# Reordering a tuned kernel: the first batch's scores and weight products, w_o's split, ScalarE's order around T1 and T2, and the end

## The chip, the cores and the metric

The kernel runs on one core of a Trainium2 chip. The metric is the time of one execution on the device in microseconds (us); less is better. A core has five engines that run their own queues of instructions in parallel: TensorE (PE: matrix products and transposes into PSUM), VectorE (DVE), ScalarE (ACT), GpSimd (POOL) and SyncE (SP, which here issues nearly all transfers). An instruction that waits holds everything behind it in its engine's queue.

## The reference, cut to what is computed

Eight batches; 8 heads of 576 tokens with 64 dimensions, 32 packed queries per head; model width 512; 4 experts of width 64, two of them chosen per token.

```python
def sm_attn(qq, kk, vv):
    a = softmax(qq @ kk.T / 8)
    return a @ vv
p_packed = sm_attn(p, k, v)                  # 32 rows per head
x = sm_attn(q, p_packed, p_packed)           # 576 rows per head, heads joined to 512

h = gelu_tanh(x @ w_in)                      # 1024 wide
u, v = h[..., :512], h[..., 512:]
v_n = (v - mean) / sqrt(var + 1e-6) * g_ln
v_s = einsum('ts,bsd->btd', w_sg, v_n) + b_sg
x = x + (u * v_s) @ w_out

w = softmax over the 2 largest of x @ w_gate
for e in range(4):
    a = causal softmax((x @ wq[e]) @ (x @ wk[e]).T / 8)
    out += w[e] * (a @ (x @ wv[e]) @ wo[e])
```

## The kernel before

**Precision.** Most products run as three passes over a high and a low part of each operand (hi by hi, hi by lo, lo by hi). Wherever a result is needed as an operand again, ACT copies the high part out of PSUM and DVE or POOL subtracts it to get the low part (`act_copy`, L82; `lo_part`, L85).

**Folding.** w_out is folded into w_qk and w_vg at the start, and the packed attention's result is carried as two factors: the 32 packed rows per head (turned: ppT) and the weights a2. So x is never formed: `bdw` (L636) multiplies the packed rows into w_qk ("bdq", the tile `bdq`) and into w_vg (`bdv`), and q, k, values and gate logits are sums of a gated part (`qk_gated`, L819: 24 products per call from gh, gl and w_qk) and a packed part (`qk_packed`, L831: 12 products from a2h, a2l and bdq). `qk_out` (L843) splits the sum. `vlog` (L860) makes values and gate logits of some token tiles.

**Batches.** `startup` (L1482) does batch 0's front half by a list of steps written out by hand (ORDER). Batch 0's back half is `first_back` (L1118), later ones' `later_back` (L1141); `back` (L1179) joins them with what is common. Each back half also carries the packed attention of the next batch in steps: K0 and K1 turn k's layout, V loads v, s0 and s1 are the scores of p with k (PE product, DVE maximum, ACT exponential; two halves of the heads), n0 and n1 their sums, a0 and a1 their transposes (PE, then a DVE copy, tile `a1t`), p0 and p1 the products with v (tile `pp`), Q0 and Q1 turn q's layout, P0 and P1 the transposed packed rows (`ppT`), and r, among others, the second scores S2 (q with the packed rows) and their softmax. `front(b)` makes v, u and the layer norm of batch b and `wp_mm` the product of the packed rows with w_in.

**Attention of the experts.** Ten items per batch (five token tiles by two pairs of experts). For item i, S is E (scores on PE, DVE's mask and maximum `nm`, ACT's exponentials, tile `at`) and N (DVE's scaling of `at`) together; T is the transposes of `at` on PE (tile `aTp`) and ACT's copies (tile `aT`). y and o, numbered by token tile, are the product with the values and the product with w_o. `vs_tile(b, m)` is the spatial product of column block m (`vs_mm`, 36 products) and `vs_out`: DVE's `gt`, ACT's high part `gh`, DVE's low part `gl`.

**Buffers.** All PSUM tiles come from one pool of four slots (`pd`, L74); a new tile waits until the readers of the oldest free slot's last tile are done. Loads of the natural layout and w_o's staging tile share two slots (`nat_slot`, L71), weights two slots "W" (w_in's halves, w_qk, w_vg), v and others three slots "a".

**What sets the order.** In the startup all five engines follow the order of the code. After it PE and SP do (L1489), and the others' order is made by the scheduler, except inside a `manual_schedule` block for an engine (VectorE's at L1159, L1197 and L1219), where the code's order holds.

**w_o.** `prep_w_o(j)` (L347) loads half of w_o through SP, copies the high part on ACT and subtracts on POOL. It is called at the end of `back(0)` (L1225), and w_o is first used by o0 of batch 0, which stands in batch 1's back half.

Of the kernel before, what the change touches and what calls it, by code (L numbers as in the profile page):

```python
# [26 lines left out]
def packed_attention_mlp_moe_kernel(  # L27
# [46 lines left out]
    def pd(name):  # L74

        return psum.tile([P, 2, 512], F32, tag="pd", name=name, bufs=NPS)
# [7 lines left out]
    def lo_part(eng, o, x, hi):  # L84
        eng.tensor_tensor(o, x, hi.bitcast(F32), op=OP.subtract)  # L85
# [291 lines left out]
    ST = {}  # L377
# [256 lines left out]
        wp_out(b, f)  # L634

    def bdw(b):  # L636

        s = ST[b]
        pt = pd("bdq")
        per_head(b, pt, 512, w_of(b, "qk"))  # L640
        for Q in range(2):
            hi, lo = s["bd", Q] = [slot("B", F32R, 512, name="bdq") for _ in range(2)]
            nc.scalar.activation(hi, pt[:, Q, :], AF.Copy)
            lo_part(nc.vector, lo, pt[:, Q, :], hi)
        pt = pd("bdv")
        per_head(b, pt, 260, w_of(b, "vg"))
        t = [slot("B", F32R, 520, name="bdv").rearrange("p (q n) -> p q n", q=2) for _ in range(2)]
        nc.scalar.activation(t[0], pt[:, :, :260], AF.Copy)
        lo_part(nc.vector, t[1], pt[:, :, :260], t[0])
        for Q in range(2):  # L650
            s["bdv", Q] = [x[:, Q, :] for x in t]
# [450 lines left out]
    def weights(b, names):  # L1102
        if b < B:
            for n in names:
                load_w(n)
# [11 lines left out]

    def first_back(b, do_all):  # L1118
        tick(len(TURN))
        do_all("K0")  # L1120
        qk_gated(b, 0, True)
        do_all("s0 n0 K1 V")
        qk_gated(b, 2, True)
        do_all("s1 n1")
        bdw(b)
        weights(b + 1, ("in1", "in0"))
        do_all("a0")
        qk_packed(b, 0, False)
        qk_out(b, 0)
        do_all("a1 p0 Q0")  # L1130
        qk_packed(b, 2, False)
        qk_out(b, 2)
        keep_last_q(b, 0)
        do_all("P0")
        vlog(b, VT[2])
        do_all("p1 Q1 P1")
        vlog(b, VT[1])
        do_all("r")
        ahead(b + 2)

    def later_back(b, go, do_all, nxt):  # L1141
        go("S1 S3")
        vs_tile(b, 0)
        vs_tile(b, 1)
        go("T1 T2 y0 S5 S4")
        vs_tile(b, 2)
        go("T3 o0 y1 T5 T4 S6 S7")
        vs_tile(b, 3)
        tick(len(TURN))
        if b + 1 < B:  # L1150
            STEP.pop((b + 1, "f"))()
        go("o1 y2")
        bdw(b)
        weights(b + 1, ("in1", "in0"))
        qk(b, 0)
        do_all("V T6 o2 T7 K0 S8 S9 K1")
        keep_last_q(b, 0)
        qk_gated(b, 2, True)
        with tc.manual_schedule(engines={ET.DVE}):  # L1159
            do_all("s0 s1 n0 n1")  # L1160
        qk_packed(b, 2, False)
        qk_out(b, 2)
        if b + 1 == B:
            go("y3 T8 T9 o3 y4")
            nxt("E8")
            go("o4")
            vlog(b, VT[1])
            nxt("E6")
            vlog(b, VT[2])
            nxt("E4")  # L1170
            return
        do_all("y3 T8 T9 o3 a0 a1 y4 p0 Q0 p1 Q1 o4 P0 P1")
        vlog(b, VT[1])
        do_all("r")
        vlog(b, VT[2])
        if b + 2 < B:
            ahead(b + 2)

    def back(b, go):  # L1179
        def do_all(names):  # L1180

            for n in names.split():
                if (b + 1, n) in STEP:
                    STEP.pop((b + 1, n))()
                elif n[0] in "STyo":
                    go(n)

        nxt = attention(b)
        if b:
            later_back(b, go, do_all, nxt)  # L1190
        else:
            first_back(b, do_all)
        vlog(b, VT[0])
        tick()
        gates(b)
        if b + 1 == B:
            with tc.manual_schedule(engines={ET.DVE}):  # L1197
                nxt("N8 N6")
                qk(b, 1)
                keep_last_q(b, 1)  # L1200
                nxt("E2 N4")
                qk_packed(b, 3, True)
                nxt("E0 N2")
                qk_gated(b, 3, False)
                qk_out(b, 3)
                nxt("N0 T8 T0 T2 E9 E1 T4 N9 E3 T6 N1 T9 y4 N3 T1 E5 y0 o4 T3 y1 N5 E7 o0 T5 y2 N7 o1 T7 y3 o2 o3")
            return
        qk(b, 1)
        keep_last_q(b, 1)
        tick()  # L1210
        nxt("E0 E2")
        qk_packed(b, 3, True)
        tick()
        qk_gated(b, 3, False, (0, 1, 2))
        wp_mm(b + 1, 1)
        wp_mm(b + 1, 0)
        qk_gated(b, 3, False, (3,))
        tick()
        with tc.manual_schedule(engines={ET.DVE}):  # L1219
            wp_out(b + 1, 1)  # L1220
            wp_out(b + 1, 0)
            qk_out(b, 3)
            nxt("N0 N2")
        weights(b + 1, ("qk", "vg"))
        if b == 0:  # L1225
            for j in range(2):
                prep_w_o(j)
        return nxt

    def ahead(b):  # L1230
# [294 lines left out]
```

## Time and profile before

| | us |
|---|---|
| median of 3 runs | 844.61 |
| lowest and highest run | 844.15 and 848.43 |
| the profiled execution's own time | 844.43 |
| span from its first to its last instruction | 842.7 |
| outside the span | 1.73 |
| mean granted clock of TensorE over the span | 0.992 |

The profile comes from one execution. Its page gives each engine's busy time; the view of waits says how long an engine stood idle in front of which instruction, and whose result came last; the timeline lists instructions in order of time, with a wait in brackets behind the instruction that waited; the view by windows gives each engine's busy time in a stretch and the clock that was granted to TensorE, as a share of 2.4 GHz. "L772" is a line of the kernel before; "x16" is a count of instructions merged into one row.

### The profile page before, as it was taken

What the parts mean: (1) busy time and instruction counts of PE and PEld (TensorE: products, weight loads), DVE (VectorE), ACT (ScalarE), POOL (GpSimd) and SP (SyncE); (2) the same over time, 40 slices, a digit from 0 to 9 for tenths busy, and PEclk for the clock granted to TensorE, in tenths of its full rate; (3) what the DMA queues carried; (4) which work ended last, traced back from release to release, by engine and by line L of the source; (5) the groups of instructions that cost most, each with busy time, mean ns of one, the idle gap of its engine ahead of it and who ended that gap; (6) DMA issues with size and microseconds to landing.
All of it is one profiled execution on the core that took longest, in us unless ns stands there. A gap on an engine that the chain in (4) does not pass through costs nothing.

```text
span 842.7 us, 19253 instructions
## 1 busy us (share of the span) xinstructions
PE 804.4 (95%) x7523; PEld 695.5 (83%) x7523; DVE 572.3 (68%) x1359; ACT 431.1 (51%) x983; POOL 226.1 (27%) x301
## 2 busy tenths in 40 slices
PE   4689989999999999999999999999999999999988
PEld 2467778788889889888889889888889889888876
DVE  5999546776468846776468856776468856775374
ACT  3655432765347542665346542665346543665344
POOL 2457412403322322303322331303322322300000
PEclk9989999999999999999999999999999999999999
DMA  9977793617555374517565475617654470200001
GB/s 249 284 202 170 221 272 92 190 50 214 141 153 121 95 231 113 165 51 217 136 163 113 101 226 112 160 56 214 147 161 108 99 228 8 76 14 27 19 1 58
DMA packets 172710, 115.00 MB, mean 136 GB/s; under 512 B 119306, under 2 KB 153610, under 8 KB 169804
## 3 DMA queue, kind: packets, MB, share of 16 engines
q1 hardware_dynamic: 165644, 112.19, 49.7%
q10 hardware_dynamic: 6976, 1.58, 0.9%
q8 instruction: 60, 0.98, 0.5%
q14 instruction: 30, 0.25, 0.1%
HBM read 69.18 MB, written 29.63 MB: 117 GB/s over the span
## 4 chain that ended last, share of the span: by engine, by line
PE 59%; DVE 14%; ACT 4%; issue 3%; ACTq 0%
PE qk L828 10%; PE vlog L871 6%; PE vs L772 6%; PE y L1011 6%; PE qk L840 6%; PE o L1060 5%; PE aTp L982 4%; PE vlog L875 3%; PE sc L924 3%; DVE vg L683 2%; DVE bnst L671 2%; DVE vnl L698 2%; PE s L392 2%; PE sc L955 2%; DVE at L943 1%
## 5 line engine op out<-in xcount | busy, mean ns | idle before, releaser
L772 PE MATMUL vs<-w_sg,vnh 128*128 128x288 f32 x512 | 91.7, 301 | 3.4 <-ACT aT L82 1.9
L473 POOL COPY kT<-kp 128x576 uint16<-128x576 uint16 x56 | 50.2, 973 | 157.6 <-DMA kp<-turned_k 132.3
L828 PE MATMUL qk<-gh,w_qk 128*128 128x288 f32 x512 | 90.6, 299 | 0.0
L772 PEld LDWEIGHTS vs<-w_sg,vnh 128*128 128x128 f32 x512 | 74.5, 188 | 10.7 <-issue 3.9
L934 ACT ACTIVATE at<-sc,nm 128x256 f32<-128x256 f32 (+3 forms) x128 | 66.1, 524 | 32.4 <-DVE nm L928 28.6
L828 PEld LDWEIGHTS qk<-gh,w_qk 128*128 128x128 f32 x512 | 74.7, 188 | 9.3 <-issue 9.3
L82 ACT ACTIVATE aT<-aTp 128x512 f32<-128x512 f32 (+4 forms) x160 | 59.3, 434 | 21.1 <-PE aTp L982 17.7
L858 POOL CAST last_q<-qk 64x64 fp32r<-64x64 f32 x64 | 14.9, 232 | 178.4 <-ACT qk L848 101.6
L871 PE MATMUL vlog<-w_vg,gh 128*128 128x260 f32 (+1 forms) x320 | 60.5, 287 | 0.0
L473 POOL COPY qT<-qp 128x576 uint16<-128x576 uint16 x56 | 42.8, 833 | 62.0 <-DMA qp<-turned_q 61.9
L1011 PE MATMUL y<-aT,v 128*64 128x128 f32 (+2 forms) x960 | 57.7, 262 | 0.2 <-DVE y L85 0.2
L679 POOL TENSOR_TENSOR rstd<-rstd,mhalf 128x1 f32<-128x1 f32 x40 | 35.5, 894 | 83.2 <-DVE rstd L675 83.2
L1011 PEld LDWEIGHTS y<-aT,v 128*64 128x64 f32 (+1 forms) x960 | 46.7, 136 | 12.2 <-issue 7.3
L943 DVE TENSOR_SCALAR at<-at,sm,gw 128x256 f32<-128x256 f32 (+3 forms) x128 | 54.8, 470 | 1.6
L828 PE MATMUL qk<-gl,w_qk 128*128 128x288 f32 x256 | 54.8, 296 | 0.0
L772 PE MATMUL vs<-w_sg,vnl 128*128 128x288 f32 x256 | 54.7, 295 | 0.0
L928 DVE TENSOR_REDUCE nm<-sc 128x2 f32<-128x256 f32 (+3 forms) x64 | 52.0, 821 | 1.5
L871 PEld LDWEIGHTS vlog<-w_vg,gh 128*128 128x128 f32 (+1 forms) x320 | 47.2, 178 | 3.9 <-DVE lg L880 2.8
L1060 PE MATMUL o<-w_o,y 128*128 128x512 f32 x186 | 50.0, 404 | 0.0
L840 PE MATMUL qk<-a2h,bdq 128*128 128x288 f32 x256 | 46.8, 305 | 0.0
L982 PE MATMUL aTp<-ident,at 128*128 128x128 f32 x320 | 43.6, 274 | 2.7 <-DVE at L943 2.3
L871 PE MATMUL vlog<-w_vg,gl 128*128 128x260 f32 (+1 forms) x160 | 45.1, 282 | 0.0
(237 smaller groups left out, 1922.9 us busy)
## 6 DMA issues: line engine op xcount, KB each, us to landing
w_in<-kept_in SPq DMA_DIRECT2D x14, 1024.0 KB
w_qk<-kept_qk SPq DMA_DIRECT2D x8, 1024.0 KB
turned_k<-kx SPq DMA_DIRECT2D x28, 288.0 KB
turned_q<-qx SPq DMA_DIRECT2D x28, 288.0 KB
kp<-turned_k SPq DMA_DIRECT2D x56, 144.0 KB
qp<-turned_q SPq DMA_DIRECT2D x56, 144.0 KB
out_dram<-ot SPq DMA_DIRECT2D x31, 256.0 KB
v<-in_v_dram SPq DMA_DIRECT2D x56, 128.0 KB
```

The costliest lines, as they stand in the source:

```text
L82: nc.scalar.activation(o, i, AF.Copy, scale=scale)
L473: nc.gpsimd.tensor_copy(w[:, i], t[:, i].rearrange("p h n -> p (h n)"))
L772: nc.tensor.matmul(pt[:, h, :], s["vn", c][x][:, cols], w_sg[y][:, c, hs(h)], start=(c, x, y) == (0, 0, 0), stop=False)
L828: nc.tensor.matmul(o[:, h, :], W["w_qk"][y][:, m, cols], s["g", m][x][:, hs(h)], start=first and (m, x, y) == (0, 0, 0), stop=not first an ...
L840: nc.tensor.matmul(o[:, h, :], s["bd", Q][y][:, cols], s["a2", Q][x][:, hs(h)], start=first and (Q, x, y) == (0, 0, 0), stop=not first and ...
L871: nc.tensor.matmul(pt[:n, ci, :260], s["g", m][x][:, c * P:c * P + n], W["w_vg"][y][:, m, :], start=(m, x, y) == (0, 0, 0), stop=False)
L928: nc.vector.tensor_reduce(nm, pt[:, :, :L], axis=AX.X, op=OP.max, negate=True)
L934: nc.scalar.activation(ats[e][:, :L], pt[:, e, :L], AF.Exp, bias=nm[:, e:e + 1], accum_out=sm[:, e:e + 1])
L943: nc.vector.tensor_scalar(ats[e][:, :L], ats[e][:, :L], sm[:, e:e + 1], s["w"][:, j, 2 * pr + e:2 * pr + e + 1], op0=OP.mult, op1=OP.mult)
L982: nc.tensor.transpose(pt[:, e, c * P:c * P + P], ats[e][:, c * P:c * P + P], ident)
L1011: nc.tensor.matmul(pt[64 * e:64 * e + 64, pr * w:pr * w + w], s["v2"][:m, c, col:col + D], s["aT", pr, e, j][c][:m, :], start=c == 0, stop ...
L1060: nc.tensor.matmul(pt, ys[:, pr, x, :], W["w_o"][y][:, pr, :], start=i == 0, stop=i == 5)
```

## The change

No arithmetic is added or removed. Five things are moved.

- `bdw` is cut in two: `bdw_qk` and `bdw_vg`.
- `first_back`: V stands ahead of K0; s0 and s1 stand directly behind one another, behind `qk_gated(0)` and K1; `bdw_qk` follows; then `qk_gated(2)`, `qk_packed(0)`, a0 and a1, `bdw_vg`, the loads of the next w_in, `qk_packed(2)`; DVE follows the written order in that stretch. p0, Q0, p1 and Q1 come ahead of the values of the last token tile, P0 and P1 behind them.
- `prep_w_o` is called at the end of `first_back`, behind r, instead of at the end of `back(0)`.
- `later_back`: ACT follows the written order in T1, T2 and `vs_out(1)`, which before was free, with `vs_out(1)` ahead of T1 in the code.
- The last batch: N0 stands ahead of `qk_out(3)`, T4 beside T2 at the front, T0 beside T6, N9 ahead of T6, E5 ahead of y4, E7 ahead of o4, N5 ahead of y1 and N7 ahead of y2.

```diff
--- before.py
+++ after.py
@@ -634,7 +634,10 @@
         wp_out(b, f)
 
     def bdw(b):
-
+        bdw_qk(b)
+        bdw_vg(b)
+
+    def bdw_qk(b):
         s = ST[b]
         pt = pd("bdq")
         per_head(b, pt, 512, w_of(b, "qk"))
@@ -642,6 +645,9 @@
             hi, lo = s["bd", Q] = [slot("B", F32R, 512, name="bdq") for _ in range(2)]
             nc.scalar.activation(hi, pt[:, Q, :], AF.Copy)
             lo_part(nc.vector, lo, pt[:, Q, :], hi)
+
+    def bdw_vg(b):
+        s = ST[b]
         pt = pd("bdv")
         per_head(b, pt, 260, w_of(b, "vg"))
         t = [slot("B", F32R, 520, name="bdv").rearrange("p (q n) -> p q n", q=2) for _ in range(2)]
@@ -1117,32 +1123,39 @@
 
     def first_back(b, do_all):
         tick(len(TURN))
-        do_all("K0")
+        do_all("V K0")
         qk_gated(b, 0, True)
-        do_all("s0 n0 K1 V")
-        qk_gated(b, 2, True)
-        do_all("s1 n1")
-        bdw(b)
-        weights(b + 1, ("in1", "in0"))
-        do_all("a0")
-        qk_packed(b, 0, False)
-        qk_out(b, 0)
-        do_all("a1 p0 Q0")
-        qk_packed(b, 2, False)
-        qk_out(b, 2)
+        do_all("K1")
+        with tc.manual_schedule(engines={ET.DVE}):
+            do_all("s0 s1")
+            bdw_qk(b)
+            do_all("n0 n1")
+            qk_gated(b, 2, True)
+            qk_packed(b, 0, False)
+            do_all("a0 a1")
+            qk_out(b, 0)
+            bdw_vg(b)
+            weights(b + 1, ("in1", "in0"))
+            qk_packed(b, 2, False)
+            qk_out(b, 2)
         keep_last_q(b, 0)
-        do_all("P0")
+        do_all("p0 Q0 p1 Q1")
         vlog(b, VT[2])
-        do_all("p1 Q1 P1")
+        do_all("P0 P1")
         vlog(b, VT[1])
         do_all("r")
+        for j in range(2):
+            prep_w_o(j)
         ahead(b + 2)
 
     def later_back(b, go, do_all, nxt):
         go("S1 S3")
         vs_tile(b, 0)
-        vs_tile(b, 1)
-        go("T1 T2 y0 S5 S4")
+        vs_mm(b, 1)
+        with tc.manual_schedule(engines={ET.Activation}):
+            go("T1 T2")
+            vs_out(b, 1)
+        go("y0 S5 S4")
         vs_tile(b, 2)
         go("T3 o0 y1 T5 T4 S6 S7")
         vs_tile(b, 3)
@@ -1202,8 +1215,9 @@
                 qk_packed(b, 3, True)
                 nxt("E0 N2")
                 qk_gated(b, 3, False)
+                nxt("N0")
                 qk_out(b, 3)
-                nxt("N0 T8 T0 T2 E9 E1 T4 N9 E3 T6 N1 T9 y4 N3 T1 E5 y0 o4 T3 y1 N5 E7 o0 T5 y2 N7 o1 T7 y3 o2 o3")
+                nxt("T8 T2 T4 E9 E1 N9 T6 T0 E3 N1 T9 E5 y4 N3 T1 y0 E7 o4 T3 N5 y1 o0 T5 N7 y2 o1 T7 y3 o2 o3")
             return
         qk(b, 1)
         keep_last_q(b, 1)
@@ -1222,9 +1236,6 @@
             qk_out(b, 3)
             nxt("N0 N2")
         weights(b + 1, ("qk", "vg"))
-        if b == 0:
-            for j in range(2):
-                prep_w_o(j)
         return nxt
 
     def ahead(b):
```

TensorE in the first batch's back half, from the first scores on, before (`w_qk_586` and `587` are the high and low part of w_qk; `a_1202` and `a_1266` the two halves' exponentials):

```order
L828 MATMUL qk<-gl,w_qk_586 128x288 x2
L392 MATMUL s_1255<-kT,pT 32x288 x8
L605 MATMUL bdq<-w_qk,ppT 32x512 x8
L605 MATMUL bdv<-w_vg,ppT 32x260 x8
L501 MATMUL a1T<-ident,a_1202 128x128 x4
L840 MATMUL qk<-a2h,bdq 128x288 x4
L840 MATMUL qk<-a2l,bdq 128x288 x2
L840 MATMUL qk<-a2h,bdq 128x288 x4
L840 MATMUL qk<-a2l,bdq 128x288 x2
L501 MATMUL a1T<-ident,a_1266 128x128 x4
L402 MATMUL pp<-v,a1t 32x64 x16
```

And the same stretch of TensorE after the change, first the scores:

```order
L834 MATMUL qk<-gl,w_qk_586 128x288 x2
L392 MATMUL s_1213<-kT,pT 32x288 x8
L392 MATMUL s_1226<-kT,pT 32x288 x8
L605 MATMUL bdq<-w_qk,ppT 32x512 x8
L834 MATMUL qk<-gh,w_qk_586 128x288 x2
```

and, behind the twelve rows of `qk_gated(2)` that this one opens, the end of the same stretch of TensorE:

```order
L834 MATMUL qk<-gl,w_qk_586 128x288 x2
L846 MATMUL qk<-a2h,bdq 128x288 x4
L846 MATMUL qk<-a2l,bdq 128x288 x2
L846 MATMUL qk<-a2h,bdq 128x288 x4
L846 MATMUL qk<-a2l,bdq 128x288 x2
L501 MATMUL a1T<-ident,a_1224 128x128 x4
L501 MATMUL a1T<-ident,a_1237 128x128 x4
L605 MATMUL bdv<-w_vg,ppT 32x260 x8
L846 MATMUL qk<-a2h,bdq 128x288 x4
```

So both scores and `bdq` now stand ahead of `qk_gated(2)`, both transposes behind `qk_packed(0)`, and `bdv` behind them; before, `bdq`, `bdv` and the first transposes stood in one row behind the second scores.

ScalarE after the change, in the first batch between the splits of q and k and the copies of the packed rows (`wst` is w_o's staging tile, `vlog` with 64 partitions the last token tile's values):

```order
L854 ACTIVATE qk<-qk 128x576
L654 ACTIVATE bdv<-bdv 128x520
L857 ACTIVATE qk<-qk 128x576
L82 ACTIVATE w_o_1561<-wst_1563 128x512
L82 ACTIVATE w_o_1561<-wst_1567 128x512
L883 ACTIVATE v_1429<-vlog 64x256
L426 ACTIVATE ppT<-ppT 128x128 x2
L883 ACTIVATE v_1429<-vlog 128x512
```

w_o's two copies, which stood between the gelus of batch 1's front before, now stand ahead of the values' copy and of both `ppT` copies. On POOL the two subtractions of w_o moved in the same way, to behind the eight copies of q's layout and ahead of the first `bt`.

ScalarE in batches 1 to 7 around the copies of T1 (128 wide) and T2 (256 wide), before (one of the batches; it reads the same in the others):

```order
L803 ACTIVATE gh<-gt 128x576
L82 ACTIVATE aT<-aTp 128x128 x2
L803 ACTIVATE gh<-gt 128x576
L82 ACTIVATE aT<-aTp 128x256 x2
L1024 ACTIVATE y<-y 128x256
```

and after:

```order
L809 ACTIVATE gh<-gt 128x576
L82 ACTIVATE aT<-aTp 128x128 x2
L82 ACTIVATE aT<-aTp 128x256 x2
L809 ACTIVATE gh<-gt 128x576
L1030 ACTIVATE y<-y 128x256
```

T2's copies changed places with the second `gh`.

TensorE in the last batch, from the transposes of item 8 on (L996; the item with the half tile), before:

```order
L996 MATMUL aTp<-ident,at 64x128
L982 MATMUL aTp<-ident,at 128x128 x6
L955 MATMUL sc<-qk,last_q_96 128x288 x4
L955 MATMUL sc<-qk,last_q_97 128x288 x2
L924 MATMUL sc<-qk 128x128 x6
L982 MATMUL aTp<-ident,at 128x128 x6
L924 MATMUL sc<-qk 128x256 x6
L982 MATMUL aTp<-ident,at 128x128 x8
L996 MATMUL aTp<-ident,at 128x128 x4
L996 MATMUL aTp<-ident,at 64x128
L1011 MATMUL y<-aT,v_10761 64x64 x20
L982 MATMUL aTp<-ident,at 128x128 x2
```

and after:

```order
L1002 MATMUL aTp<-ident,at 64x128
L988 MATMUL aTp<-ident,at 128x128 x10
L961 MATMUL sc<-qk,last_q_96 128x288 x4
L961 MATMUL sc<-qk,last_q_97 128x288 x2
L930 MATMUL sc<-qk 128x128 x6
L988 MATMUL aTp<-ident,at 128x128 x10
L930 MATMUL sc<-qk 128x256 x6
L1002 MATMUL aTp<-ident,at 128x128 x4
L1002 MATMUL aTp<-ident,at 64x128
L930 MATMUL sc<-qk 128x384 x6
L1017 MATMUL y<-aT,v_10785 64x64 x20
L988 MATMUL aTp<-ident,at 128x128 x2
```

T4's six transposes went to the front beside T2's, T0's two behind E1, and the scores of E5 (384 wide) came ahead of y4.

## Rows read from the trace of the kernel before

**Rows 1.** The page: engine, busy time, share of the span, instructions.

```profile
PE 804.4 (95%) x7523; PEld 695.5 (83%) x7523; DVE 572.3 (68%) x1359; ACT 431.1 (51%) x983; POOL 226.1 (27%) x301
```

**Rows 2.** Waits of PE: instruction, releaser, total us, times, longest us.

```profile
PE aTp L982 <- DVE at L943: 2.3, 2, 1.7
PE a1T L501 <- DVE bdq L85: 2.1, 1, 2.1
PE vs L772 <- ACT aT L82: 1.9, 6, 0.3
...
PE vs L776 <- DVE vnh L700: 1.4, 1, 1.4
...
PE bdv L605 <- ACT a L481: 0.9, 1, 0.9
...
PE u L742 <- ACT u L749: 0.7, 1, 0.7
PE aTp L996 <- DVE at L968: 0.7, 1, 0.7
PE ppT L421 <- DVE pp L416: 0.7, 1, 0.7
...
PE aTp L982 <- ACT aT L82: 0.4, 1, 0.4
```

**Rows 3.** Timeline of PE in the first batch: start, us, instruction, [wait ahead].

```profile
108.68 0.71 PE L392 MATMUL s<-kT,pT 64*32 64x288 f32 x16
...
112.70 0.72 PE L392 MATMUL s<-kT,pT 64*32 64x288 f32 x16
113.21 1.06 PE L605 MATMUL bdq<-w_qk,ppT 64*32 64x512 f32 x16
115.20 0.67 PE L605 MATMUL bdv<-w_vg,ppT 64*32 64x260 f32 x16 [0.93 <-ACT a L481]
...
117.96 1.09 PE L501 MATMUL a1T<-ident,a 128*128 128x128 f32 x4 [2.09 <-DVE bdq L85]
118.70 1.31 PE L840 MATMUL qk<-a2h,bdq 128*128 128x288 f32 x4
...
122.81 0.79 PE L840 MATMUL qk<-a2h,bdq 128*128 128x288 f32 x4
```

**Rows 4.** Windows: us; PE, PEld, DVE, ACT, POOL; PEclk, DMA share, GB/s.

```profile
117.00:122.00 5.00, 4.04 (x28) 3.90 (x32) 2.01 (x4) 0.98 (x3) 0.00 (x0) 0.66 1.04 316
```

**Rows 5.** Timeline of DVE in the first batch: the copy of turned scores.

```profile
119.09 0.69 DVE L503 COPY a1t<-a1T 128x512 f32<-128x512 f32 x1 [0.67 <-PE a1T L501]
```

**Rows 6.** Timeline of SP: the issue of w_qk's load for `bdq`.

```profile
103.95 0.47 SPq L196 DMA_DIRECT2D w_qk<-kept_qk  x1
```

**Rows 7.** Timeline of batch 1's front: w_o's loads, its split, and DVE beside it.

```profile
150.97 1.00 SPq L351 DMA_DIRECT2D wst<-in_moe_wo_dram  x2
...
157.09 1.37 ACT L82 ACTIVATE w_o<-wst 128x512 fp32r<-128x512 f32 x2 [1.22 <-DMA wst<-in_moe_wo_dram]
...
157.80 3.31 POOL L85 TENSOR_TENSOR w_o<-wst,w_o 128x512 fp32r<-128x512 f32 x2 [6.61 <-ACT w_o L82]
161.08 1.06 POOL L679 TENSOR_TENSOR rstd<-rstd,mhalf 128x1 f32<-128x1 f32 x2
...
157.52 0.75 DVE L683 SCALAR_TENSOR_TENSOR vg<-vg,mv,g_bc 128x512 f32<-128x512 f32 x1
...
158.25 1.72 DVE L683 SCALAR_TENSOR_TENSOR vg<-vg,mv,g_bc 128x512 f32<-128x512 f32 x1
```

**Rows 8.** Timeline of ACT in a later batch: the second `gh` and T2's copies.

```profile
272.27 0.69 ACT L803 ACTIVATE gh<-gt 128x576 fp32r<-128x576 f32 x1 [0.83 <-DVE gt L795]
272.86 0.64 ACT L82 ACTIVATE aT<-aTp 128x256 f32<-128x256 f32 x2
```

**Rows 9.** Timeline of ACT in the last batch: T6's copies, E5's exponential.

```profile
818.21 1.11 ACT L82 ACTIVATE aT<-aTp 128x512 f32<-128x512 f32 x2
...
825.27 0.58 ACT L934 ACTIVATE at<-sc,nm 128x384 f32<-128x384 f32 x1
```

## The prediction

> **What bounds the kernel now.** I read the page first: TensorE is busy for 804.4 us, 95% of the span, and no other engine passes 68% [rows 1]. The change takes no product away, so it can only shorten TensorE's idle time, or the time it runs below full clock. I then read the view of waits for PE: what matters there is where each wait lies and how often it comes. Four groups lie in the places the change touches [rows 2]: in the first batch 0.9 (`bdv`), 2.1 (the turned scores a1T) and 0.7 (`ppT`); in batch 1's front 0.7 (u) and 1.4 (vs, L776), neither of which occurs in later batches; 1.9 in six batches, 0.3 each, where the third spatial product waits for a copy of `aT`; and in the end 2.3 and 0.7 for `at`, and 0.4 for `aT`. The timeline then shows what each one hangs on, and the windows show the granted clock. The sum is made against the profiled execution's 844.43, which is 0.18 below the median 844.61; its span is 842.7.
>
> **The change part by part.**
>
> *First batch.* Before, the second scores s start at 112.70, `bdq` at 113.21, and `bdv` at 115.20 after 0.93 of waiting, because its PSUM slot is freed only by the exponential of those scores: 2.50 from the scores' start to the free slot. Then a1T waits another 2.09 for the slot of `bdq`, which ACT and DVE must split first [rows 3]. With `ppT`'s 0.7 [rows 2] that is 0.93 + 2.09 + 0.69 = 3.71 of idle time. TensorE's clock falls behind it: the granted clock is 0.66 on average in 117 to 122 [rows 4], so part of that stretch ran at 1.2 GHz and not 2.4, after the two waits. The first four products of `qk_packed(0)` take 1.31, the same four of `qk_packed(2)` 0.79 [rows 3]. That is 0.52 at least; all of the window's loss is 5.00 x 0.34 = 1.70. The low stretch covers more than those four, a third of the call, so I take 1.2.
>
> What takes their place: s0, s1 and `bdq` now follow one another, with s costing 0.51 (112.70 to 113.21) and `bdq` 1.06 [rows 3]. `qk_gated(2)` behind them takes the slot of s0 and waits for s0's exponential: 2.50 less 2.08 of work ahead of it, **0.42**. ACT's and DVE's splitting of `bdq`, which made a1T wait, is then hidden behind `qk_gated(2)`'s 24 products. `bdv` needs the slot of the first half's a1T, which DVE frees by a copy of 0.69 [rows 5]; beside it stand the second half's four transposes, at most 0.74 (117.96 to 118.70 at the low clock, [rows 3]), about half of which at full clock. This wait lies between 0 and 0.7; I take 0.35. The copies and splits on DVE stand in written order: a1t's two copies ahead of the low part of q, which nobody needs before the first attention. P0 and P1, behind the values of the last token tile, no longer wait for `pp`; those 18 products cover it.
>
> `bdq` also comes earlier, and needs w_qk. The first scores started at 108.68 [rows 3]; two of them later, at 109.70, `bdq` now starts, and w_qk's load is issued at 103.95 [rows 6], 5.75 ahead. Before, `bdq` began at 113.21 without a wait for it, so the wait lies between 0 and 3.5. The nearest row with both ends is w_o's: issued at 150.97 behind other loads, its copy could start at 157.09 [rows 7], 6.1 later. With that w_qk is 0.4 late, and those 0.4 only take the place of the 0.42 above: I add nothing, and carry up to 0.6 in the range.
>
> Sum of this term: 3.71 + 1.2 - 0.42 - 0.35 = **4.1** (2.0 with all bounds against it, 5.0 with none).
>
> *w_o.* In batch 1's front ACT waits 1.22 for w_o's data, copies for 1.37, and POOL subtracts for 3.31, until 161.1, ahead of the layer norm's `rstd` (161.08) [rows 7]; vnh is made from that, and TensorE waits 0.7 and 1.4 [rows 2]. Without w_o in those queues I expect both gone: 2.1. In its new place w_o's loads stand on SP behind the two w_in halves, and need the two slots of natural layout, free once the first `pp` product has read v. The copies stand on ACT ahead of the last token tile's values and both `ppT` copies, and S2 on PE needs `ppT`. By the gain above S2 comes 4.1 earlier. The copies take 1.37 [rows 7] and stand beside some 4 us of value products, so they are free unless the data comes late; with 6.1 from issue to landing the second half is late by about 0.2. POOL's 3.31 lie between q's layout and S2's first `bt`, where POOL had nothing to do. Taken: **1.9**; bounds 2.1, and -1.0 where the transfers come 3 us later than that.
>
> One row speaks against it: while POOL subtracted w_o, a scaling on DVE (L683) took 1.72 rather than 0.75 [rows 7], and the same POOL work now lies beside DVE's work for `ppT`, so up to 0.97 could return there. The Trainium skill ("GPSIMD Engine Reference", section 1, Specifications) says that GpSimd and VectorE share their interfaces to SBUF, and that VectorE's instructions with two inputs in SBUF contend for them. L683 has two such inputs, which agrees; the `pp` scaling and the split of k read PSUM, so by that rule nothing returns, and by the row taken alone the sum would be 0.97 less.
>
> *T1 and T2.* The third spatial product waits 0.32 in six batches for the slot that T2's copies free. On ACT they stand behind the second `gh`, which itself waits 0.83 for DVE [rows 8]. With the order turned round T2's copies can go where ACT stood idle, for 0.64, and end about 0.7 ahead of when TensorE asks. The second `gh` is later by little, as DVE's `gt` releases it at 272.27 while T2's copies would be done by 272.1. Six times 0.32: **1.9**. Bounds: 0, if the wait only moves to the next item, and 2.2.
>
> *End.* Removed: 2.3 (1.73 because N0 stood on DVE behind the split that `qk_out(3)` starts, and 0.56 because N7 stood behind y's split), 0.7 and 0.4 [rows 2], 3.4 together. New by the written order: E3 asks for a PSUM slot that E9's exponential holds, 0.6; T9 for one behind T6's two copies, which take 1.11 [rows 9], less what lies beside, 0.6; y0 stands directly behind T1 now, while ACT has E5's two exponentials of 0.58 [rows 9] ahead of T1's copies: 1.16 and half of the 0.64 that copies of twice the width take [rows 8], less y0's first products, 1.25. That is 2.45, and the gain **0.9** (bounds 2.5 and -1.0).
>
> Sum: 4.1 + 1.9 + 1.9 + 0.9 = 8.8, so 844.43 - 8.8 = **835.6**.
>
> **The rivals.**
>
> *w_o late* (chance 0.12). ACT is held by a copy without data, and both `ppT` copies and S2 stand behind it. Against it speaks the 6.1 above, for it that more than 2 MB of w_in stand ahead in the same queue. With 3 us more than I took: 835.6 + 3.0 = 838.6.
>
> *The first batch's wait comes back elsewhere* (0.10). The slots are as many as before, and if w_qk or an exponential is late, `qk_gated(2)` waits for 2 us and the clock falls again: 2 + 1.2, so 838.8. For it: `bdq` is asked for 3.5 us earlier.
>
> *T1 and T2 only move the wait* (0.07). DVE gets the second `gl` later, y1 and T3 wait in its place: 835.6 + 1.9 = 837.5.
>
> *SP's queue* (0.02, slower). V's loads now stand ahead of K0's remaining layout work on SP, in order, and the first of them waits for a slot "a". If that slot came free late, everything behind it, w_qk's load too, would slide, and `bdq` with it one for one after the 0.4. It decides from 9.3 us of delay on (8.8 plus 0.4): with 10 us the time is 835.6 + 9.6 = 845.2. Against it: SP issued w_qk at 103.95 [rows 6], and that slot's last reader, a conversion of w_in, stands in the middle of the startup's list.
>
> *The first batch does nothing* (0.02): the scheduler's order leaves the waits in place, 835.6 + 4.1 = 839.7.
>
> **How the numbers follow.** 0.67 for the forecast, with 0.12, 0.10, 0.07, 0.02 and 0.02 for the others. The lower end has every wait named above vanish and nothing in its place: about 832.5. The upper end takes in the first three rivals, and two of their prices together: 840.2. About 0.5%, here 4.2 us, is what a measurement of this kernel can tell from no change: 840.2 is that border too. Past it, but within 0.5%, lie the worse thirds of the four rivals that lose part of the gain and sums of them, together 0.10; only SP's queue can pass 848.7, with a delay of 14 us or more, and I give the 0.02 of it to slower as a whole. Faster by over 0.5%: 0.88; within: 0.10; slower: 0.02.
>
> **What would show it.** In the changed kernel's profile: no wait over 0.6 on PE between the first scores and S2, and a granted clock of 1.00 in each window there; no wait for w_o on ACT over 1 us, and no wait in front of u or vs in batch 1; no 0.3 in front of the third spatial product; at the end waits of about 2.5 in all. Wrong it would be if ACT stands in front of w_o's copy while PE waits for `ppT`, if `bdq` waits for w_qk, or if T3's or y1's wait has grown by what T2's lost.

## The result, and the profile after

| | before | changed |
|---|---|---|
| median, us | 845.9 (4 runs, 844.15 to 848.43) | 835.36 (4 runs, 832.84 to 836.75) |
| ratio, 95% interval | | 0.9862 (0.9833 to 0.9892) |
| profiled execution, us | 844.43 | 836.55 |
| its span, us | 842.7 | 834.8 |

The changed kernel is faster by 1.4%, clear of noise; 835.6 was forecast, with a range of 832.5 to 840.2. The ratio is not the quotient of the two medians, which is 0.9875: between the medians the gain is 10.5, by the ratio 11.7 (interval 9.1 to 14.1). The profiled execution of the changed kernel is the second slowest of its four, and that of the kernel before lies 1.5 below the median of its runs, so the two traces show less of the gain than the ratio.

The page's first line, in the columns of [rows 1]:

```profile
PE 802.2 (96%) x7523; PEld 693.3 (83%) x7523; DVE 571.7 (68%) x1359; ACT 429.1 (51%) x983; POOL 228.0 (27%) x301
```

TensorE does the same 7523 instructions; the span is shorter, so its share rose. Its waits, in the columns of [rows 2]:

```profile
PE s L392 <- ACT ppT L426: 1.8, 1, 1.8
...
PE y L1017 <- ACT aT L82: 0.9, 1, 0.9
...
PE sc L930 <- ACT at L967: 0.7, 1, 0.7
PE bdq L605 <- DVE st L479: 0.5, 1, 0.5
...
PE aTp L1002 <- ACT aT L82: 0.5, 1, 0.5
...
PE bdv L605 <- DVE a1t L503: 0.3, 1, 0.3
```

All nine waits of [rows 2] are gone. A new one, 1.8 in front of S2 (`s` from `ppT`), was forecast only as a rival. The timeline of PE in the first batch, against [rows 3]:

```profile
109.82 1.20 PE L392 MATMUL s<-kT,pT 64*32 64x288 f32 x32
111.54 1.09 PE L605 MATMUL bdq<-w_qk,ppT 64*32 64x512 f32 x16 [0.52 <-DVE st L479]
...
117.46 1.03 PE L501 MATMUL a1T<-ident,a 128*128 128x128 f32 x8
118.84 0.67 PE L605 MATMUL bdv<-w_vg,ppT 64*32 64x260 f32 x16 [0.35 <-DVE a1t L503]
...
131.83 1.21 PE L392 MATMUL s<-qT,ppT 64*32 64x288 f32 x32 [1.83 <-ACT ppT L426]
```

S2 starts at 131.83, 22.01 behind the first scores. Before, it was 24.40 behind the first scores at 108.68 (PE's timeline before):

```profile
133.08 1.20 PE L392 MATMUL s<-qT,ppT 64*32 64x288 f32 x32
```

What holds S2 now is on ScalarE (first SP's issue of w_o's loads, then ScalarE's rows):

```profile
121.92 0.86 SPq L351 DMA_DIRECT2D wst<-in_moe_wo_dram  x2
```

```profile
129.94 1.31 ACT L82 ACTIVATE w_o<-wst 128x512 fp32r<-128x512 f32 x2 [7.95 <-DMA wst<-in_moe_wo_dram]
131.16 0.36 ACT L883 ACTIVATE v<-vlog 64x256 f32<-64x256 f32 x1
131.43 0.42 ACT L426 ACTIVATE ppT<-ppT 128x128 f32<-128x128 f32 x2
```

The loads were issued at 121.92, and the first copy could run at 129.94, 8.0 later, where before it took 6.1 [rows 7]. ScalarE stood still for 7.95 with `ppT`'s copies behind it.

To compare executions whose startup runs at different speeds, I cut every trace at the starts of the second scores S2 (the `s<-qT,ppT` rows of PE's timeline):

| stretch, us | before | changed |
|---|---|---|
| first scores s0 to S2, batch 0's back half | 24.40 | 22.01 |
| from there to the next S2 (batch 1's front in it) | 94.68 | 92.06 |
| the five stretches that follow, mean | 94.54 | 94.13 |
| last S2 to the span's end | 142.26 | 140.24 |

Unrounded, the means differ by 0.40. That is 2.39 + 2.62 + 5 x 0.40 + 2.02 = 9.0; the startup up to s0 was 1.14 slower in the changed kernel's execution (109.82 against 108.68), which leaves the 7.9 between the spans.

### The profile page after: what moved, and what is told of

Same layout as the page of the kernel before. It is cut to its first block, busy times and chain, and to the rows that moved or that the text cites. A ratio compares the mean times of both kernels' runs of the same rounds, so it can differ in the third digit from the quotient of the medians.

```text
span 834.8 us, 19249 instructions
## 1 busy us (share of the span) xinstructions
PE 802.2 (96%) x7523; PEld 693.3 (83%) x7523; DVE 571.7 (68%) x1359; ACT 429.1 (51%) x983; POOL 228.0 (27%) x301
## 4 chain that ended last, share of the span: by engine, by line
PE 81%; DVE 8%; DMA 6%; ACT 2%; issue 1%; SPq 1%; ACTq 0%; POOL 0%; DVEq 0%; POOLq 0%
PE vs L778 11%; PE qk L834 11%; PE y L1017 7%; PE vlog L877 6%; PE qk L846 6%; PE v L667 6%; PE u L748 5%; PE o L1066 5%; PE sc L930 4%; PE aTp L988 4%; PE vlog L881 3%; PE s L392 2%; PE sc L961 2%; PE aTp L1002 1%; DVE wpl L85 1%
```

## The experiments

Ratios are to runs of the kernel before, made on the same chip in the same job. The runs were made in three jobs: the parts alone, then two sets of four. The kernel before took 847.2, 845.7 and 846.3 in them, and the times in the expectations start from 844.4, so ratios and places are compared and not those times. Each trace is of one execution; where that one is the slowest or the fastest of its run, this is said.

### Each part alone

The first batch's order, on the kernel before: `bdw` cut in two and `first_back` as in the change, but

```diff
         do_all("r")
-        for j in range(2):
-            prep_w_o(j)
         ahead(b + 2)
```

> The first batch's new order alone; w_o's split, ScalarE's order around T1 and T2 and the end as before. I read one place: the start of the second scores S2 of batch 0's back half, 133.08 us before, 131.83 in the changed kernel (there behind a wait of 1.83 for the turned rows ppT, which ScalarE holds behind w_o's copies). Theory A (the order's gain is real, w_o's copies take part of it away, and V's loads, now ahead of K0 on SP, delay k's layout by some 2 us): S2 starts at 130.0, without a wait over 0.5 for ppT, and the kernel takes about 841.5. Theory B (as forecast, V's place costs nothing): S2 at 129.0, 840.5. Theory C (the order gives nothing, what S2 gained was a startup that happened to run faster): S2 at 132.3 or later, 843.8.

Measured: 842.19 (10 runs), ratio 0.9956 (0.9936 to 0.9975). The profiled execution is the slowest of the ten (845.02). In it S2 started at 133.69, and 24.27 behind s0, which reads like theory C. But something else had come in (PE's timeline):

```profile
113.86 1.16 PE L605 MATMUL bdq<-w_qk,ppT 64*32 64x512 f32 x16 [3.24 <-DMA w_qk<-kept_qk]
```

and SP's issue of that load:

```profile
106.10 0.47 SPq L196 DMA_DIRECT2D w_qk<-kept_qk  x1
```

w_qk was issued at 106.10, and `bdq` could start 7.8 later, having waited 3.24 for it; the windows show a granted clock of 0.78 in 112 to 117 and 0.88 in 117 to 122. Against an execution of the same order in which w_qk was in time (below, S2 19.85 behind s0), the wait put the products behind `bdq` 3.0 later and the low clock another 1.4. The order itself gains (the ratio is clear of 1), and in this execution the transfer takes the gain back. Of theory A the part on V falls: its reason, SP issuing k's layout some 2 us later, is seen in the next runs too, where V has its old place (93.13 and 94.44 in the runs of the end and of T1 and T2 alone; 93.67 in this one, 93.46 in the changed kernel; 91.15 before). That execution of the kernel before had a fast startup.

w_o's split moved, in the old order:

```diff
         do_all("r")
+        for j in range(2):
+            prep_w_o(j)
         ahead(b + 2)
@@ back
         weights(b + 1, ("qk", "vg"))
-        if b == 0:
-            for j in range(2):
-                prep_w_o(j)
```

> w_o's split in the first batch alone, in the old order of that batch. Places: S2 of batch 0's back half (133.08 before), and from there to S2 of batch 1's (94.68 before, 92.06 in the changed kernel, of which 0.43 is T1 and T2's). Theory A (w_o's transfers come late, and what stands behind its copies on ScalarE waits; batch 1 gains 2.2): S2 later than 134.5, the next stretch 92.5, the kernel at 844.5 to 845.5, no gain by itself. Theory B (as forecast, the copies are free): S2 at 133.1 or 133.3, 842.5. Theory C (w_o was not what held batch 1's layer norm): the next stretch stays at 94.7.

Measured: 847.41 (10 runs), ratio 1.000 (0.9978 to 1.0022). The profiled execution is the slowest of the ten (852.13), so the loss that it shows is an extreme. The stretch behind S2 fell to 92.07, so batch 1 gained 2.6, and S2 came 31.45 behind s0, 7.05 later than before. ScalarE's rows show where:

```profile
133.24 0.63 ACT L82 ACTIVATE w_o<-wst 128x512 fp32r<-128x512 f32 x1 [7.64 <-DMA wst<-in_moe_wo_dram]
133.78 0.63 ACT L851 ACTIVATE qk<-qk 128x576 fp32r<-128x576 f32 x1
```

and PE's:

```profile
120.37 0.67 PE L605 MATMUL bdv<-w_vg,ppT 64*32 64x260 f32 x16 [2.91 <-DMA w_vg<-kept_vg]
...
136.34 0.45 PE L421 MATMUL ppT<-ident,pp 128*128 128x128 f32 x1 [5.11 <-DVE pp L416]
```

w_o's copy waited 7.64 for data, the high part of k stood behind it on ScalarE, on DVE the low part of k and the `pp` scaling behind that, and PE lost 5.11, where it lost 0.69 before. Compared start by start with the kernel before (each product's start behind s0 against that of the same product there), 4.4 of the 7.05 come at this `ppT` and 2.5 behind it, in the products up to S2, where the windows show granted clocks of 0.80 (132 to 137) and 0.52 (137 to 142). `bdv`'s wait for w_vg costs nothing: it takes the place of a1T's 2.09, and a1T starts 9.28 behind s0 in both. Theory A's mechanism holds; over the ten runs, by the ratio, the loss in batch 0 is as large as the gain in batch 1.

T1 and T2 alone:

```diff
-        vs_tile(b, 1)
-        go("T1 T2 y0 S5 S4")
+        vs_mm(b, 1)
+        with tc.manual_schedule(engines={ET.Activation}):
+            go("T1 T2")
+            vs_out(b, 1)
+        go("y0 S5 S4")
```

> ScalarE's written order around T1 and T2 alone. Place: the stretch from one batch's S2 to the next in batches 2 to 6, 94.55 before and 94.12 in the changed kernel. Theory A (this part alone took 0.43 per batch): 94.12, and the kernel at 842.0. Theory B (as forecast, 0.32 per batch): 94.23, 842.7. Theory C (the wait only moves): 94.5, 844.4.

Measured: 844.38 (9 runs), ratio 0.9962 (0.9943 to 0.9981). The stretches are 94.13, and the last one 141.92, 0.34 less. Theory A: 5 x 0.40 + 0.34 = 2.3. The rows of ScalarE in the changed kernel, in the columns of [rows 8]:

```profile
267.95 0.66 ACT L82 ACTIVATE aT<-aTp 128x256 f32<-128x256 f32 x2 [0.41 <-PE y L1017]
...
268.50 0.69 ACT L809 ACTIVATE gh<-gt 128x576 fp32r<-128x576 f32 x1
```

T2's copies run in time that ScalarE stood idle in before, `gh` directly behind them, and no wait of PE is left in a whole stretch.

The end alone:

```diff
+                nxt("N0")
                 qk_out(b, 3)
-                nxt("N0 T8 T0 T2 E9 E1 T4 N9 E3 T6 N1 T9 y4 N3 T1 E5 y0 o4 ...
+                nxt("T8 T2 T4 E9 E1 N9 T6 T0 E3 N1 T9 E5 y4 N3 T1 y0 E7 o4 ...
```

> The last batch's new order alone. Place: from the last S2 to the span's end, 142.26 before, 140.24 in the changed kernel, of which 0.43 should be T1 and T2's. Theory A (the end's part is 1.6): 140.7, and the kernel at 843.0. Theory B (as forecast): 141.4, 843.7. Theory C (the end's gain needs the split of w_o or T1 and T2): 142 or more, 844.6. Waits of PE in the end: about 2.1 in all by A, 2.5 by B.

Measured: 844.45 (10 runs), ratio 0.9972 (0.9956 to 0.9989); the last stretch 140.75, so 1.5 less: theory A. The waits left in the end, in the changed kernel's timeline of PE:

```profile
809.29 0.62 PE L930 MATMUL sc<-qk 64*128 64x256 f32 x6 [0.66 <-ACT at L967]
810.39 0.74 PE L1002 MATMUL aTp<-ident,at 128*128 128x128 f32 x5 [0.48 <-ACT aT L82]
...
815.27 0.60 PE L1017 MATMUL y<-aT,v 128*64 128x128 f32 x4 [0.93 <-ACT aT L82]
```

This run also measures the clock's price in the first batch, whose order is the old one here. PE's rows and the windows (columns as in [rows 4]):

```profile
116.30 0.67 PE L605 MATMUL bdv<-w_vg,ppT 64*32 64x260 f32 x16 [0.93 <-ACT a L481]
119.07 0.63 PE L501 MATMUL a1T<-ident,a 128*128 128x128 f32 x4 [2.09 <-DVE bdq L85]
```

```profile
117.00:122.00 5.00, 2.93 (x44) 2.79 (x48) 2.70 (x5) 1.74 (x3) 0.00 (x0) 1.00 1.17 231
```

The two waits are those of [rows 3], to the hundredth, but the granted clock stayed at 1.00, here and in the windows beside it, where [rows 4] has 0.66. S2 came 23.07 behind s0, against 24.40: the low clock cost 1.33 in the kernel before, all of it within 3.1 us of a1T's start, and it is not there in every execution. (It was in the run with T1 and T2 alone: 0.87 and 0.78 in 117 to 127, S2 at 24.62.)

### Where w_o's copies and w_qk's load stand

w_o's copies behind both `ppT` copies on ScalarE, the loads as they were, on the changed kernel:

```diff
-        do_all("P0 P1")
+        with tc.manual_schedule(engines={ET.Activation}):
+            do_all("P0 P1")
+            for j in range(2):
+                prep_w_o(j)
         vlog(b, VT[1])
         do_all("r")
-        for j in range(2):
-            prep_w_o(j)
```

> The changed kernel with w_o's two copies behind both ppT copies in ScalarE's written order; its loads stay where they are. Place: from the start of the first batch's first scores s0 to S2, 22.01 us in the changed kernel (24.40 before, 23.07 in the run with the new end alone). Theory A (w_o's data comes late, and ScalarE holds the ppT copies behind it): no wait for ppT, the place takes 20.2 plus whatever bdq waits, the stretch from that S2 to the next stays at 92.1, and the kernel is 1.8 faster than the changed one, ratio to the kernel before about 0.984. Theory B (w_o's late data then holds the second scores' exponentials on ScalarE in the same way): S2 as in A, but the next stretch 93.5 or more, and the kernel as the changed one. Theory C (S2 waits for something else anyway, such as q's layout): the place stays at 22.0.

Measured: 836.18 (6 runs), ratio 0.9889 (0.9856 to 0.9922). No wait for `ppT`; S2 20.91 behind s0, of which `bdq` waited 1.35 for w_qk; the next stretch 92.06. That is theory A's trace. But this is the fastest of the six, and w_o landed early in it (127.42), so the trace can't tell A from B. The ratio of 0.984 that A named lies outside the interval.

w_qk's load ahead of the four v loads, on the changed kernel (`G` is those loads, taken out of the step `F`):

```diff
-        gl3 gl0 W fh3 gl2 fl3
+        gl3 gl0 Wq G Wv fh3 gl2 fl3
```

> The changed kernel with w_qk's load ahead of the four v loads and their rests that stand in front of it on SP. Place: bdq's start less s0's start, 1.72 in the changed kernel, 4.44 with the first batch's order alone (there 3.24 of waiting for w_qk), 1.2 if nothing holds it. Theory A (w_qk is late because SP issues it late, which differs between executions): no wait for w_qk in front of bdq, at most the 0.5 for DVE's maximum, spread of the times smaller, and the median about 1 faster than the changed kernel. Theory B (it is late because the transfer engines are full; issue order doesn't matter): waits of 1 to 3 stay in some executions, the median is unchanged. In both the wait of 1.8 for ppT stays.

Measured: 838.62 (6 runs), ratio 0.9907 (0.9878 to 0.9936). w_qk was issued at 103.91 and not 106.30, and `bdq` started 0.99 behind s0 and waited for nothing: A on that point. The median is not faster. In the profiled execution, the slowest of the six (841.12), w_o's loads were issued at 123.94, its data came at 132.45, and S2 waited 4.41 for `ppT`:

```profile
134.28 2.18 PE L392 MATMUL s<-qT,ppT 64*32 64x288 f32 x32 [4.41 <-ACT ppT L426]
```

These 32 products took 2.18 and not 1.21: the granted clock was 0.52 in 132 to 137. The stretch behind S2 took 94.17 and not 92.1, and all of these 2.1 were lost in its first 5 us. So late data costs more than the row of the wait shows.

Both together (the two edits above in one kernel):

> Both: w_o's copies behind the ppT copies, and w_qk's load ahead of the v loads. If both first theories hold: s0 to S2 20.2, no wait over 0.6 between them, 2.8 faster than the changed kernel, ratio to the kernel before about 0.983. If the second theories hold: as the changed kernel.

Measured: 837.44 (6 runs), ratio 0.9893 (0.9867 to 0.992). S2 19.80 behind s0, without a wait, and yet the kernel is not faster: the next stretch took 94.75 instead of 92.1. First ScalarE, then DVE, then PE of this run:

```profile
131.26 1.24 ACT L82 ACTIVATE w_o<-wst 128x512 fp32r<-128x512 f32 x2 [5.28 <-DMA wst<-in_moe_wo_dram]
132.41 0.58 ACT L889 ACTIVATE v<-vlog 128x512 f32<-128x512 f32 x1
```

```profile
133.02 0.17 DVE L892 COPY lg<-vlog 128x8 f32<-128x8 f32 x1 [7.01 <-ACT v L889]
133.20 0.85 DVE L522 STREAM_TRANSPOSE bt<-s 128x288 f32<-128x288 f32 x2
```

```profile
141.86 0.80 PE L852 MATMUL qk<-a2h,bdq 128*128 128x288 f32 x4 [0.89 <-DVE lg L892]
```

Here w_o landed at 131.26. Behind its copies stood the copy of the values, behind that DVE's gate logits `lg`, and behind them in DVE's queue the turning of S2's scores, with which the softmax begins. S2 itself was on time, at 129.61, and this `lg` copy 3.4 behind it; in the run with w_o's copies alone behind `ppT`, where w_o was in time, S2 stood at 129.34 and `lg` at 130.07, 0.7 behind. PE paid for it with this 0.89 and three waits of 0.4 to 0.5 in front of wp and v. So theory B holds in this execution, where the data was late: the copies' place on ScalarE chose who waits. With w_qk's load moved, w_o's loads were also issued later: 13.0 and 14.0 behind s0 in these two executions, 11.9 and 12.1 in the two of the changed kernel.

w_o's move undone, the rest of the change as it is:

```diff
         do_all("r")
-        for j in range(2):
-            prep_w_o(j)
         ahead(b + 2)
@@ back
         weights(b + 1, ("qk", "vg"))
+        if b == 0:
+            for j in range(2):
+                prep_w_o(j)
```

> The changed kernel with w_o's load and split back at the end of the first back half, the rest as changed. Theory A (the move cost 1.8 in front of S2 and gave 2.6 in batch 1): no wait for ppT, s0 to S2 20.2 plus bdq's wait, the stretch behind it 94.7, and the kernel 0.8 slower than the changed one. Theory B (as forecast, the copies were nearly free in their new place): 1.9 slower. Theory C (the move cost more than it gave, as the run with w_o alone had it on the whole): as fast as the changed one or faster.

Measured: 838.32 (6 runs), ratio 0.9905 (0.9878 to 0.9931). In the profiled execution, the slowest of the six, the stretch behind S2 is 94.69, with the waits of 0.5 (u) and 1.4 (vs) back, and `bdq` waited 2.88 for w_qk. This set has no run of the changed kernel beside it, so its theories are settled by the last run below.

### The changed kernel again, and w_o's loads ahead of w_in

The changed kernel once more, unedited:

> The changed kernel once more, beside the next three. Theory A (its time moves by when w_o's and w_qk's transfers land, which differs between executions): median 835 to 838, ratio to the kernel before 0.985 to 0.990, a wait for ppT in front of S2 between 0.5 and 4.5, one for w_qk between 0 and 3.3. Theory B (the first result was typical): 835.4, 0.986.

Measured: 834.8 (4 runs), ratio 0.9861 (0.984 to 0.9882). In this execution w_o landed in time, and the first batch is what the forecast drew. PE:

```profile
111.97 0.79 PE L834 MATMUL qk<-gh,w_qk 128*128 128x288 f32 x4 [0.44 <-ACT a L481]
...
118.25 0.67 PE L605 MATMUL bdv<-w_vg,ppT 64*32 64x260 f32 x16 [0.35 <-DVE a1t L503]
...
129.32 1.20 PE L392 MATMUL s<-qT,ppT 64*32 64x288 f32 x32
```

and ScalarE:

```profile
126.54 1.28 ACT L82 ACTIVATE w_o<-wst 128x512 fp32r<-128x512 f32 x2 [5.14 <-DMA wst<-in_moe_wo_dram]
127.72 0.36 ACT L883 ACTIVATE v<-vlog 64x256 f32<-64x256 f32 x1
127.99 0.42 ACT L426 ACTIVATE ppT<-ppT 128x128 f32<-128x128 f32 x2
```

w_o was issued at 121.32 and its copy ran at 126.54, 5.2 later; `ppT` was copied by 128.4, ahead of S2 at 129.32. S2 stands 19.85 behind s0. The time is theory B's; of A the premise is seen (w_o's data took 5.2 here and 8.0 in the first execution), its slower time is not.

w_o's loads ahead of the two w_in halves, staged in two slots of the tag "T" (free then), its copies behind `ppT`:

```diff
             bdw_vg(b)
+            for j in range(2):
+                load_w_o(j)
             weights(b + 1, ("in1", "in0"))
@@
-        st = nat_slot(F32, "wst2")
+        st = slot("T", name="wst2")
```

> The changed kernel with w_o's loads ahead of the two w_in halves on SP, staged in slots that are free then (of the tiles for aT), and its copies on ScalarE behind both ppT copies. Theory A (w_o is late because 2 MB of w_in stand ahead of it, and what it holds on ScalarE is first ppT, then the copy of the values and through DVE's queue the second scores' softmax): w_o's data lands before 125, no wait of ScalarE for it, no wait for ppT, batch 1's stretch 92.1, and the median 2 to 3 faster than the changed kernel. Theory B (w_in comes 0.5 MB later and is then the late one): a wait for wp or v in batch 1 of about 1, the gain at most 1.

Measured: 835.31 (4 runs), ratio 0.9862 (0.984 to 0.9884). w_o's copies wait for nothing any more:

```profile
126.00 0.42 ACT L429 ACTIVATE ppT<-ppT 128x128 f32<-128x128 f32 x2
126.31 1.15 ACT L82 ACTIVATE w_o<-wst 128x512 fp32r<-128x512 f32 x2
```

The next stretch is 92.06 and nothing is late in batch 1, so theory B's late w_in did not come. S2 was 20.47 behind s0, with 0.94 of waiting for w_qk. The median, though, is that of the changed kernel, and not the 2 to 3 faster of theory A: what w_o's late data costs the changed kernel on the whole is not shown.

With w_qk's load moved as well:

> As the last one, and w_qk's load ahead of the four v loads on SP. Theory A (both transfers are late by their place in SP's order): no wait over 0.6 from s0 to S2, that stretch 20.0, batch 1's 92.1; 0.5 to 1.5 faster than the last one, the fastest of the four, and the spread of its times the smallest. Theory B (moving w_qk gives nothing on the whole, as in the two runs with it so far): as the last one.

Measured: 834.01 (4 runs), ratio 0.9852 (0.9831 to 0.9873); from s0 to S2 19.81 with 0.44 and 0.35 as the only waits, then 92.05. It is the lowest median and the lowest ratio of all, but its interval covers the changed kernel's, and its runs (832.84 to 836.42) spread as the others do. That it beats the changed kernel is not shown.

w_o's move undone, once more, in the same job:

> The changed kernel with w_o's load and split back at the end of the first back half, once more, on the chip of the changed kernel. Theory A (the move gives 2.6 in batch 1 and costs what S2 waits for ppT): slower than the changed kernel by 2.6 less that wait, 0.5 to 1.5. Theory B (as forecast): 1.9 slower.

Measured: 837.97 (6 runs), ratio 0.9906 (0.9885 to 0.9927), against 0.9861 for the changed kernel: 3.2 between the medians; the profiled execution is the fastest of the six. The intervals just fail to overlap, and the job before gave 0.9905 for the same kernel. The stretch behind S2 is 94.76 here, 92.08 there, with both waits of batch 1 back (0.57 at u, 1.39 at vs). By the traces the move is worth 2.6 less what S2 waits. That is theory A's mechanism; its 0.5 to 1.5 supposed a wait at S2, which this job's profiled execution of the changed kernel doesn't have. B's 1.9 is within the intervals too: the size is not told apart, the place and the sign are.

## Why the prediction was right

The terms, read from the traces:

| term | forecast, us | measured | from |
|---|---|---|---|
| first batch | 4.1 | 4.55 less what w_qk and w_o make late | 24.40 - 19.85 |
| w_o out of batch 1 | 1.9 | 2.6 | 94.68 - 92.07 |
| T1 and T2 | 1.9 | 2.3 | 5 x 0.40 + 0.34 |
| end | 0.9 | 1.5 | 142.26 - 140.75 |

**First batch: right.** The new waits were put at 0.42 and 0.35 and measure 0.44 and 0.35; the clock's price was put at 1.2 and measures 1.33 where it falls. In both profiled executions of the changed kernel the granted clock is 1.00 in every window from 107 to 132, as forecast. (The term's lower bound of 2.0 doesn't follow from the figures named for it: 3.71 + 0.52 - 0.42 - 0.7 - 0.6 is 2.5.) All of the old waits went, and a1T waits for nothing, as `qk_gated(2)` covers the split of `bdq`.

**w_qk: a step that failed.** I counted 5.75 us from w_qk's issue to `bdq`'s turn, from one execution of the kernel before [rows 3, 6], took 6.1 for the transfer and let the rest vanish behind the 0.42. In the seven profiled executions with the new order and w_qk in its old place, `bdq`'s turn (1.0 behind s0) comes 3.7 to 4.6 us after the issue in five and 5.4 and 5.6 in two, since SP is later against TensorE in most. That is not peculiar to the new order: in the three other executions of the old order w_qk was issued 3.0 to 3.8 ahead of s0, in these seven 2.7 to 4.6 ahead, in the one that I read 4.7. From the issue to `bdq`'s start it takes 5.1 to 7.8 in the five. So `bdq` waited 0.52, 0.94, 1.35, 2.88 and 3.24 in them and not in the two; in the three with the load issued earlier (103.3 to 103.9) it did not wait either. The 0.52 is the changed kernel's, where the row names DVE's maximum; but `bdq` doesn't need that, and in the changed kernel's second execution (s0 at 109.47) it starts before the maximum is done, so I read it as w_qk's. The second rival forecast a wait of 2 us and a lower clock: such a wait is in two of the seven (2.88 and 3.24), the lower clock only in that with 3.24, the run of this order alone; with 2.88 the windows show 1.00.

**w_o late: the mechanism of the first rival, in some executions.** I took 6.1 us from issue to landing and 0.2 of waiting. Measured, with the copies ahead of `ppT`: 5.2 and no wait, 8.0 and 1.83, 8.5 and 4.41 (there issued later too, at 123.94). I gave the rival 3 us with a chance of 0.12; it is rather a cost that some executions pay and others don't. Two of the prediction's own signs of being wrong are thus in the changed kernel's first trace: ScalarE stands in front of w_o's copy while PE waits for `ppT`, and `bdq` waits, by the reading above, for w_qk.

**Batch 1: right, under-sized.** The waits of 0.74 and 1.38 went, and the stretch fell by 2.6, not 2.1 at the most. Compared start by start, all of it lies at these two places, 0.97 at u and 1.65 at vs, so the rows of waits count less than the stops cost. The row that spoke against the move found nothing to slow: in the changed kernel's second execution POOL subtracts w_o from 127.3 to 129.8, and the `pp` scaling, done by 123.1, takes 1.02, as without w_o there (1.03). So whether POOL caused L683's 1.72 stays untested. In the execution without late data PE waits for nothing in front of S2, and behind it, up to batch 1's vs, only 0.27 (for wpl, which is there before too).

**T1 and T2: right, under-sized.** The wait of 0.32 is worth 0.40: compared start by start in batch 2, the product behind it starts 0.42 earlier and nothing else moves by more than a few hundredths. The wait did not move to T3 or y1.

**End: right, under-sized.** Forecast were 0.6 (E3), 0.6 (T9) and 1.25 (y0), in all 2.45; they came at just these places with 0.66, 0.48 and 0.93, in all 2.07.

**SP and V: not seen.** SP issues k's layout at 91.2 to 95.9 in the four executions with V in its old place and at 91.9 to 93.9 in the ten with V ahead.

So that the time of 835.6 came out to 0.2 is in part luck: two errors cancel. I subtracted 8.8 from 844.43, the time of one execution. The kernel before measured 845.9 in the result, 1.5 more, and the gain between the medians is 10.5, 1.7 more. The gain itself was under-sized: 8.8 lies just below the ratio's interval of 9.1 to 14.1. The terms read from the traces add up to 4.55 + 2.6 + 2.3 + 1.5 = 11.0 where nothing is late, and what late transfers take back of it on the whole is not shown. The parts alone give 0.0044 + 0 + 0.0038 + 0.0028 = 0.011 against 0.0138 for the whole, which intervals of 0.002 to 0.003 each do not tell apart. The sharper comparison is of w_o's move: 0 alone in the old order, 3.2 between the medians in the new one. In the old order's trace its loads were issued 14.1 behind s0, in the new one's 11.9 and 12.1; that this is the reason is not shown.

What stays open is why w_o's transfer takes 5.2 in one execution and 8.0 in another with the same order on SP, and w_qk's 5.1 or 7.8. The windows show some 285 to 360 GB/s in 117 to 127 in both cases. That 2 MB of w_in stand ahead in the queue is not shown to be the reason either: with w_o's loads ahead of w_in and w_qk's moved, the second copy still waited 0.15 for its data, 6.3 behind the issue of the first load (120.45). No run here tells apart what else the transfer engines had to do.

## What to carry to other kernels

Before a step is moved to a quiet place, ask of every transfer that it issues how long such a transfer took in the worst row, not in the one at hand, and who stands behind its first reader in that engine's queue: moving w_o's copies behind `ppT` gave the wait, in the execution where the data was late, to the values' copy and, by DVE's queue, to the softmax. And parts that gain nothing alone may pay together, so a part is to be judged by taking it out of the whole as well as by putting it in alone.

## What the runs showed of the hardware that was not expected

The time from a load's issue to the first use of its data differs much between executions of the same program. For w_qk (1 MB) it was 7.6 in one execution of the kernel with w_o's move undone and at most 5.6 in another; for w_o (two loads of 256 KB) 8.0 and 5.2 in the two of the changed kernel.

TensorE's granted clock did not fall at the same place each time. Behind the same two waits of 0.93 and 2.09 it was 0.66 on average over 5 us in the kernel before, and 1.00 in the run with the new end alone.
